# Regrouped units, casting transfers from GpSimd and a new placement in a linear-attention kernel with a bilinear feed-forward

## The chip, the cores and the metric

The kernel runs on one core of one Trainium2 chip, alone. The metric is the device time of one execution in microseconds (us). The engines are named as in the profile: PE (TensorE), DVE (VectorE), ACT (ScalarE), POOL (GpSimd) and SP, which issues transfers.

## The reference, cut to what matters

```python
# q, k, v: (4, 8, 768, 64); lam: (8,)
for b in range(12):                       # blocks of 64 positions
    intra = einsum(qb, kb) * Dmask        # lam ** (i - j) below the diagonal
    intra = einsum(intra, vb)
    inter = einsum(qb * lam_pow, kv_state)
    out[block] = intra + inter
    kv_state = lam_block * kv_state + einsum(kb * rev_pow, vb)
x = out.transpose(0, 2, 1, 3).reshape(3072, 512)
return ((x @ w_a) * (x @ w_b)) @ w_out    # w_a, w_b: 512 x 1536; w_out: 1536 x 512
```

Inputs and output are float32; the kernel computes in bf16 with float32 sums.

## The kernel before, in words

The 3072 tokens are 24 units of 128 tokens, six for each of the four batches. For each unit the kernel loads q, k and v (256 KB each, in rows of 64 numbers), scales q and k by powers of lam (`qk`), turns them (`qkT`, on PE in `piece_T` or by a transposing transfer), makes the scores `kq` of its eight heads in two PSUM banks, multiplies them by a triangular mask into `m`, and adds `m` times v and the running state times q into `o_ps` (`pieces_O`). A copy to `xT` ends the attention of a unit (`evac_o`). The running state `kvd` is kept in PSUM over a batch and copied to `st`. The first four units are loaded packed and handled together at the start (`scale4`, `part_k`, `natural_k`, `scores4`).

The feed-forward works on groups of units, `GROUPS = (4, 1, 2, 4, 4, 4, 4, 1)`. A plain group (`ffn`) makes for each of twelve 128-column chunks f the product with w_a (`a_ps`), copies it to bf16 (`a_sb`), makes the product with w_b (`b_ps`), multiplies both into `ab`, and then multiplies `ab` with w_out (`op`). A group in `Z_GROUPS` (`ffn_z`) uses a scheme with seven half-size products instead of eight. It needs sums of the weights (`wz`, `weight_sum`), sums of `xT` (`x_sums`: `z_sub`, `z_add`, `z_mix`), three combining subtractions on DVE per output pair, copies `u` on ACT, and one product `ab <- oab` per pair. A group in `ZO_GROUPS` also makes the output product in this way (`ab_sum`, `out_half`, 14 halves per group), and these halves run while the next group is in its first product.

The weights come as 18 chunks of 512 KB (six each of w_a, w_b, w_out; `load_w`), are staged in float32 in buffers that later hold other things, and are cast to bf16 by DVE, ACT or POOL (`cast_w`). `pump` issues, on SP's queue, the next transfer for which a buffer is free, in one fixed order for weights and units.

Each engine runs its instructions in program order. That order is written out by hand: the group functions call `hook(slot)` after certain steps, and the table `PLAN` names the pieces that are issued at each slot (P: scale q, k and cast v; T: turn; S: scores and masks; V: state; O2: outputs of two units; X: sums of xT; SM and H: parts of the seven-product output; WS, WO, C: weight sums and casts). Tables such as `SUM_ENG` and `MASK_ACT` choose the engine. An instruction waits on semaphores for what it reads and for the buffers it overwrites, and everything behind it on its engine waits too.

Of the kernel before, what the change touches and what calls it, by code (L numbers as in the profile page):

```python
# [22 lines left out]
def _bc(ap, dims):  # L23
# [4 lines left out]
GROUPS = (4, 1, 2, 4, 4, 4, 4, 1)  # L28
W_CHUNKS = (256,) * 6
W_STEPS = ((0, 1), (2,), (3,), (4, 5))  # L30
W_HALVES = (4, 5)
LOOKAHEAD = {9: 2, 10: 1}
DMA_T = range(7, 24)
KEEP_GROUPS = 2
PACK = 4

PLAN = {
    0: [(7, 'C', 0), (8, 'C', 1), (17, 'C', 2), (18, 'WS', 0), (19, 'WS', 1), (20, 'V', 3),
        (21, 'PK', 4), (22, 'C', 3), (23, 'T', 4), (25, 'C', 4), (27, 'C', 5), (28, 'PV', 4),
        (29, 'WS', 2), (29, 'PK', 5), (31, 'S', 4), (33, 'O', 4), (34, 'WS', 3),
        (35, 'WS', 4), (35, 'V', 4)],
    1: [(0, 'PV', 5), (0, 'WS', 5), (3, 'T', 5), (4, 'PK', 6), (6, 'PV', 6), (9, 'P', 7),
        (11, 'S', 5), (11, 'T', 6), (12, 'S', 6), (13, 'P', 8), (13, 'O2', (5, 6)),
        (13, 'WS', 6), (13, 'WS', 7)],
    2: [(0, 'V', 6), (2, 'W', None), (2, 'W', None), (3, 'P', 9), (4, 'V', 7), (4, 'S', 7),  # L50
        (6, 'V', 8), (10, 'PK', 10), (11, 'PV', 10), (11, 'P', 11), (11, 'W', None),
        (11, 'S', 8), (11, 'P', 12), (12, 'Q', (7, 8, 9, 10)), (13, 'P', 13),
        (13, 'W', None), (13, 'V', 9), (14, 'O2', (9, 10)), (14, 'X', 3), (15, 'W', None)],
    3: [(1, 'S', 11), (5, 'S', 12), (8, 'O2', (11, 12)), (10, 'P', 14), (12, 'S', 13),
        (15, 'P', 15), (17, 'WO', 0), (17, 'S', 14), (18, 'V', 13), (18, 'WO', 1),
        (19, 'P', 16), (19, 'O2', (13, 14)), (20, 'P', 17), (21, 'S', 15), (21, 'P', 18),
        (24, 'WO', 2), (25, 'WO', 3), (25, 'WO', 4), (25, 'X', 4)],
    4: [(0, 'S', 16), (1, 'V', 15), (3, 'S', 17), (4, 'O2', (15, 16)), (4, 'P', 19),
        (6, 'P', 20), (6, 'S', 18), (10, 'O2', (17, 18)), (10, 'X', 5), (11, 'S', 19),
        (13, 'P', 21), (16, 'SM', (4, 0)), (17, 'SM', (4, 2)), (17, 'P', 22), (17, 'S', 20),  # L60
        (17, 'SM', (4, 4))],
    5: [(0, 'SM', (4, 1)), (1, 'H', (4, 0)), (1, 'V', 19), (2, 'O2', (19, 20)),
        (2, 'H', (4, 1)), (3, 'SM', (4, 3)), (4, 'H', (4, 2)), (5, 'S', 21), (5, 'V', 21),
        (6, 'S', 22), (6, 'H', (4, 3)), (7, 'SM', (4, 5)), (7, 'H', (4, 4)),
        (8, 'H', (4, 5)), (9, 'P', 23), (9, 'H', (4, 6)), (9, 'SM', (4, 6)),
        (10, 'SM', (4, 7)), (10, 'H', (4, 7)), (11, 'H', (4, 8)), (11, 'S', 23),
        (12, 'H', (4, 9)), (12, 'SM', (5, 0)), (12, 'H', (4, 10)), (13, 'SM', (5, 2)),
        (13, 'H', (4, 11)), (14, 'O2', (21, 22)), (16, 'H', (4, 12)), (17, 'X', 6),
        (17, 'H', (4, 13)), (17, 'SM', (5, 4))],
    6: [(0, 'SM', (5, 1)), (0, 'O', 23), (1, 'H', (5, 0)), (1, 'SM', (5, 3)),  # L70
        (2, 'H', (5, 1)), (4, 'H', (5, 2)), (5, 'H', (5, 3)), (6, 'SM', (5, 5)),
        (7, 'H', (5, 4)), (7, 'SM', (5, 6)), (8, 'H', (5, 5)), (9, 'SM', (5, 7)),
        (9, 'H', (5, 6)), (10, 'H', (5, 7)), (11, 'H', (5, 8)), (13, 'H', (5, 9)),
        (14, 'H', (5, 10)), (14, 'SM', (6, 0)), (15, 'H', (5, 11)), (15, 'SM', (6, 2)),
        (15, 'SM', (6, 4)), (16, 'H', (5, 12)), (17, 'H', (5, 13))],
    7: [(0, 'H', (6, 0)), (0, 'SM', (6, 1)), (0, 'H', (6, 1)), (0, 'SM', (6, 3)),
        (0, 'SM', (6, 5)), (0, 'H', (6, 2)), (1, 'H', (6, 3)), (3, 'H', (6, 4)),
        (4, 'H', (6, 5)), (5, 'SM', (6, 6)), (5, 'SM', (6, 7)), (5, 'H', (6, 6)),
        (6, 'H', (6, 7)), (6, 'H', (6, 8)), (6, 'H', (6, 9)), (7, 'H', (6, 10)),
        (8, 'H', (6, 11)), (10, 'H', (6, 12)), (10, 'H', (6, 13))],  # L80
}
Z_GROUPS = (3, 4, 5, 6)
ZO_GROUPS = (4, 5, 6)
FIN_AT = 5
N_LATE = 3
EV_ENG = {(u, b): "act" for u in range(24) for b in range(2)}
MASK_ACT = dict(enumerate([0] * 7 +
                        [1] +
                        [0] * 3 +
                        [1] * 2 +  # L90
                        [0] * 4 +
                        [1] * 3 +
                        [0] +
                        [1] +
                        [0] * 2))
KV_ENG = dict(enumerate(["dve"] * 10 + ["act"] * 2 + ["dve"] + ["act"] * 11))
VB_ENG = dict(enumerate(["pool"] * 7 +
                        ["dve"] * 3 +
                        ["pool"] * 5 +
                        ["dve"] * 2 +  # L100
                        ["act"] +
                        ["pool"] +
                        ["dve"] +
                        ["pool"] +
                        ["act"] * 3))
SUM_ENG = {(3, 0): 'dve', (3, 1): 'dve', (3, 2): 'pool', (3, 3): 'dve', (3, 4): 'pool', (3, 5): 'pool', (3, 6): 'dve', (3, 7): 'dve', (4, 0): 'dve', (4, 1): 'pool', (4, 2): 'pool', (4, 3): 'pool', (4, 4): 'dve', (4, 5): 'pool', (4, 6): 'pool', (4, 7): 'pool', (5, 0): 'dve', (5, 1): 'dve', (5, 2): 'pool', (5, 3): 'pool', (5, 4): 'dve', (5, 5): 'pool', (5, 6): 'pool', (5, 7): 'dve', (6, 0): 'pool', (6, 1): 'dve', (6, 2): 'pool', (6, 3): 'dve', (6, 4): 'dve', (6, 5): 'pool', (6, 6): 'dve', (6, 7): 'dve'}
XS_ENG = {(3, 0): 'dve', (3, 1): 'dve', (3, 2): 'dve', (4, 0): 'dve', (4, 1): 'dve', (4, 2): 'dve', (5, 0): 'dve', (5, 1): 'pool', (5, 2): 'pool', (6, 0): 'pool', (6, 1): 'pool', (6, 2): 'pool'}
WS_ENG = {0: 'dve', 1: 'dve', 2: 'dve', 3: 'dve', 4: 'dve', 5: 'dve', 6: 'dve', 7: 'pool'}
WO_ENG = {0: 'dve', 1: 'dve', 2: 'pool', 3: 'dve', 4: 'dve'}
CO_ENG = {0: 'pool', 1: 'pool', 2: 'pool', 3: 'dve', 4: 'dve', 5: 'dve'}  # L110
# [3 lines left out]
def kernel(  # L114
# [40 lines left out]
    raw_pool = ctx.enter_context(tc.tile_pool(name="raw", bufs=1))  # L155
# [16 lines left out]
    def z_bank(name, i):  # L172
        return ps_pool.tile([128, 2, 256], F32, name=name, tag=f"ps{i}")
# [5 lines left out]
    raw = {}  # L179

    def load_x(w, u):
        b, nb = divmod(u, NB)
        if w == "v" and u == GROUPS[0] - 1:
            t = o_pool.tile([128, H, D], F32, name="vf", tag="osb")
        else:
            t = ld_pool.tile([128, H, D], F32, name=w + "f", tag=w + "f")
        nc.sync.dma_start(out=t, in_={"q": qr, "k": kr, "v": vr}[w][b, nb])
        raw[u, w] = t
# [7 lines left out]
    staged = {}  # L196
    HN, NP = d_model // 2, FC // 2

    def sum_tile(shape, dt, name, tag):
        return sum_pool.tile(shape, dt, name=name, tag=tag)  # L200

    ab_stage = ab_pool.tile([128, 3, 1024], F32, name="wst", tag="ab")
    slots = [lambda: oab_pool.tile([128, 1024], F32, name="wst", tag="oab")] * 2
    slots += [lambda i=i: ab_stage[:, i] for i in range(3)]
    slots += [lambda t=t: sum_tile([128, 1024], F32, "wst", t) for t in ("zab", "wy0", "wy1")]
    once = lambda: xT_pool.tile([128, 1024], F32, name="wst", tag="xT")
    slots.insert(0, once)
# [8 lines left out]
    def load_w(kind, c):  # L216
        slot = slots.pop(0)
        t = slot()
        if kind == "o":
            t = t.rearrange("p (k n) -> p k n", k=2)  # L220
            nc.sync.dma_start(out=t, in_=wo_r[:, 2 * c:2 * c + 2, :])
        else:
            w = W_CHUNKS[c]
            t = t[:, :KS * w].rearrange("p (k n) -> p k n", k=KS)
            r = wa_r if kind == "a" else wb_r
            if c in W_HALVES:
                t = t.rearrange("p k n -> p (k n)").rearrange("p (k n) -> p k n", k=2)
            nc.sync.dma_start(out=t, in_=w_part(r, c))
        staged[kind, c] = t, slot

    def cast_w(kind, c, eng):
        t, slot = staged.pop((kind, c))
        if slot is not once:
            slots.append(slot)
        if kind == "o":
            dst = wo_sb[:, 2 * c:2 * c + 2, :]
        else:
            dst = w_part(wa_sb if kind == "a" else wb_sb, c)
        if eng == "act":
            nc.scalar.copy(dst, t)  # L240
        elif eng == "pool":
            nc.gpsimd.tensor_copy(dst, t)
# [59 lines left out]
    def pump():  # L302
        while pending:
            kind, c = pending[0]
            if kind in "abo":
                if not slots:
                    return
# [771 lines left out]
```

## Time and profile before

| | |
|---|---|
| times of three runs | 225.08, 225.38, 226.76 us; median 225.38 |
| span of the profiled execution | 224.7 us |
| PE busy, matmuls | 214.6 us, 2235 |
| DVE, ACT, POOL busy | 164.8, 123.2, 101.1 us |
| packets and bytes of all transfers | 99081, 39.42 MB |
| granted PE clock | 1.00 in all slices |

The profile gives the span of one execution, from the first instruction to the last; what lies around it is the difference to the measured time, some 0.7 us against the median. Busy time counts the union of an engine's instructions. Matmuls overlap in the pipeline, so that the distance between the starts of two of them, not the length of one, is PE's pace.

### The profile page before, as it was taken

To read this page: it belongs to the slowest core of one execution; us is meant where nothing else is said; L and a number is where in the kernel's file an instruction comes from. 1 tells how busy PE (TensorE), PEld (TensorE's weight loads), DVE (VectorE), ACT (ScalarE), POOL (GpSimd) and SP (SyncE) were. 2 spreads that over 40 slices of the span, in tenths; PEclk is the share of its full clock that TensorE was granted. 3 is DMA by queue.
4 is the path that set the end of the run, shared out by engine and by line. 5 is a ranking of instruction groups with operands and counts; after the bars stand their busy time and mean duration, and the time that the engine had idled before them with its cause. 6 is when DMAs were issued, how large, how long until landed. Compare 5 with 4: busy or idle time off the path is not lost.

```text
span 224.7 us, 5609 instructions
## 1 busy us (share of the span) xinstructions
PE 214.6 (96%) x2235; PEld 158.8 (71%) x2235; DVE 164.8 (73%) x269; ACT 123.2 (55%) x251; POOL 101.1 (45%) x95
## 2 busy tenths in 40 slices
PE   7699999989989999999999999899999999999994
PEld 2375444437768757887547878688888888887994
DVE  1895673599699659989878999968686765777440
ACT  3586446017544247775366988776536665533322
POOL 6061004256895075541459359786417722052000
PEclk9999999999999999999999999999999999999999
DMA  4999999998999999999999999652021100112042
GB/s 137 316 231 356 356 384 346 276 217 192 229 198 218 219 180 240 204 253 247 175 240 243 243 206 202 138 98 48 2 88 55 50 1 4 47 48 95 0 143 93
DMA packets 99081, 39.42 MB, mean 175 GB/s; under 512 B 85488, under 2 KB 95088, under 8 KB 99056
## 3 DMA queue, kind: packets, MB, share of 16 engines
q1 hardware_dynamic: 98768, 39.00, 78.0%
q8 instruction: 17, 0.28, 0.5%
q10 hardware_dynamic: 288, 0.07, 0.1%
q14 instruction: 8, 0.07, 0.1%
HBM read 28.32 MB, written 6.29 MB: 154 GB/s over the span
## 4 chain that ended last, share of the span: by engine, by line
PE 80%; DVE 6%; DMA 6%; ACT 3%; issue 2%; SPq 1%; ACTq 0%; DVEq 0%
PE U L730 17%; PE op L852 12%; PE b_ps L596 9%; PE op L643 8%; PE V L730 8%; PE a_ps L596 8%; PE op L792 5%; PE W L730 4%; DMA wst<-in_moe_w_b_dram 4%; PE o_ps L497 3%; DMA k<-in_k_dram 3%; PE kq L457 2%; PE kvd L527 1%; SPq L350 1%; DVE m L480 1%
## 5 line engine op out<-in xcount | busy, mean ns | idle before, releaser
L811 ACT COPY u<-U 128x512 f32<-128x512 f32 x48 | 28.4, 591 | 16.9 <-PE U L730 16.6
L401 POOL TENSOR_TENSOR qk<-kf,lp_k 128x512 bf16<-128x512 f32 x18 | 19.8, 1099 | 34.6 <-DMA kf<-in_k_dram 23.1
L623 DVE TENSOR_TENSOR ab<-a_sb,b_ps 128x128 bf16<-128x128 bf16 (+2 forms) x48 | 19.2, 417 | 14.0 <-ACT a_sb L605 11.1
L480 DVE TENSOR_TENSOR m<-kq,lotri 128x512 bf16<-128x512 f32 x40 | 25.7, 684 | 3.8 <-PE kq L457 3.6
L596 PE MATMUL a_ps<-xT,wa_sb 128*128 128x128 bf16 (+2 forms) x200 | 27.8, 268 | 0.6 <-ACT xT L520 0.5
L596 PE MATMUL b_ps<-xT,wb_sb 128*128 128x128 bf16 (+2 forms) x192 | 27.5, 272 | 0.7 <-ACT oab L736 0.5
L738 DVE TENSOR_TENSOR ab<-oab 128x1024 bf16<-128x1024 bf16 x24 | 18.4, 767 | 10.5 <-ACT oab L736 10.5
L401 POOL TENSOR_TENSOR qk<-qf,lp_q 128x512 bf16<-128x512 f32 x20 | 25.2, 1259 | 1.2 <-DMA qf<-in_q_dram 1.2
L605 ACT CAST a_sb<-a_ps 128x128 bf16<-128x128 f32 (+2 forms) x48 | 17.1, 375 | 14.4 <-PE a_ps L596 14.3
L643 PE MATMUL op<-wo_sb,ab 128*128 128x512 bf16 (+2 forms) x120 | 22.8, 337 | 0.2 <-DVE wo_sb L254 0.2
L596 PEld LDWEIGHTS <-wa_sb 128*128 128x128 bf16 x200 | 16.6, 98 | 6.6 <-issue 0.7
L596 PEld LDWEIGHTS <-wb_sb 128*128 128x128 bf16 x192 | 15.7, 98 | 7.3 <-DVE wb_sb L251 0.7
L730 PEld LDWEIGHTS <-wz_a 128*128 128x128 bf16 x192 | 18.2, 98 | 3.6 <-issue 0.7
L730 PEld LDWEIGHTS <-wz_b 128*128 128x128 bf16 x192 | 18.7, 98 | 2.2
L730 PE MATMUL U<-xT,wz_a 128*128 128x256 bf16 x96 | 18.3, 272 | 0.0
L730 PE MATMUL U<-xT,wz_b 128*128 128x256 bf16 x96 | 18.3, 272 | 0.0
L520 ACT CAST xT<-o_ps 128x512 bf16<-128x512 f32 (+1 forms) x24 | 12.2, 556 | 10.7 <-PE o_ps L497 10.5
L420 POOL CAST vb<-vf 128x512 bf16<-128x512 f32 x14 | 10.9, 778 | 13.9 <-DMA vf<-in_v_dram 13.9
L769 DVE TENSOR_TENSOR oab<-U,u 128x512 bf16<-128x512 f32 x24 | 16.4, 682 | 0.4 <-PE U L730 0.4
L730 PEld LDWEIGHTS <-wa_sb 128*128 128x128 bf16 x144 | 13.4, 97 | 4.5 <-issue 1.7
L643 PEld LDWEIGHTS <-ab 128*128 128x128 bf16 x120 | 10.1, 98 | 8.6 <-issue 0.3
L736 ACT CAST oab<-U 128x512 bf16<-128x512 f32 x24 | 14.2, 591 | 3.6 <-PE U L730 3.5
(126 smaller groups left out, 453.8 us busy)
## 6 DMA issues: line engine op xcount, KB each, us to landing
vf<-in_v_dram SPq DMA_DIRECT2D x24, 256.0 KB, 4.8
qf<-in_q_dram SPq DMA_DIRECT2D x20, 256.0 KB, 4.6
kf<-in_k_dram SPq DMA_DIRECT2D x20, 256.0 KB, 4.6
out_dram<-o_sb SPq DMA_DIRECT2D x18, 256.0 KB, 2.5
wst<-in_moe_w_a_dram SPq DMA_DIRECT2D x6, 512.0 KB, 8.5
wst<-in_moe_w_b_dram SPq DMA_DIRECT2D x6, 512.0 KB, 9.0
wst<-in_moe_w_out_dram SPq DMA_DIRECT2D x6, 512.0 KB, 10.6
out_dram<-o_kept SPq DMA_DIRECT2D x5, 256.0 KB, 4.4
```

What stands on the lines that cost most here:

```text
L401: eng_of(eng).tensor_mul(dst.rearrange("p (c b) d -> p b c d", b=2), x[:].rearrange("p (b c) d -> p b c d", b=2), lp.rearrange("p (b c) o ...
L480: nc.vector.tensor_mul(m, kq[i], lotri_bc)
L596: nc.tensor.matmul(ps[:, lo:hi], lhsT=w_sb[:, s, f * 128:(f + 1) * 128], rhs=xT[:, s, lo:hi], start=(s == 0), stop=(s == KS - 1), skip_gro ...
L605: nc.scalar.copy(a_sb[:, :gt], ps[:, :gt])
L623: nc.vector.tensor_mul(ab[:, f, :gt], a_sb[:, :gt], ps[:, :gt])
L643: nc.tensor.matmul(op[:, lo:hi], lhsT=ab[:, f, t * 128:(t + 1) * 128], rhs=wo_sb[:, f, lo:hi], start=(f == 0), stop=(f == FC - 1))
L730: nc.tensor.matmul(ps[:, k, :], lhsT=wt[:, s, n * 128:(n + 1) * 128], rhs=rhs[i][:, s, :], start=(fresh and k == 0 and s == 0), stop=True, ...
L736: nc.scalar.copy(oab[:, 0], U)
L738: nc.vector.tensor_mul(ab[:].rearrange("p (h i) (t c) -> p h i t c", h=2, t=2)[:, :, n], o5[:, :, :, 0, :], o5[:, :, :, 1, :])
L769: nc.vector.tensor_sub(oab[:, 1], U, v1)
L811: nc.scalar.copy(t, ps)
L852: nc.tensor.matmul(ps[:, t, :], lhsT=lhs[p][:, n, t * 128:(t + 1) * 128], rhs=rhs[:, n, :], start=fresh, stop=True, skip_group_check=True)
```

## The change

- The groups become 4, 1, 3, 4, 4, 4, 4 units. The group of three units uses the seven-product scheme for a and b (with 192-column operands) and the plain output product; the four groups of four use it for both. No plain group stands at the end. The plain group of one unit packs four chunks into each PSUM bank.
- Weights go straight from float32 in memory to bf16 in place, by transfers that cast, issued by POOL (`load_w`); only the first two chunks of w_a still come as float32 on SP's queue and are cast by ACT and POOL (`load_first`, `cast_first`). v of units 4 to 23 comes in the same way as bf16 (`load_x`); v of units 0 to 3 is cast by DVE or POOL. There is no staging and no `pump`: each load is a piece with a place of its own.
- In the first group the products of chunks 0 and 1 are made in two halves, for units 0, 1 and units 2, 3 (`ffn_first`).
- Loads of q and k for units 4 to 6 wait for a one-element memset on DVE (`GATED`).
- Every piece is placed anew, also those of the first four units: `PLAN` has entries for the start (-1) and for each group, with up to 6 slots per output pair (3 before), and finer pieces (LQ, LK, LV, LW: loads; PK, PQ: scaling; TR: turn; S, M: scores, masks; V, K: state and its copy; O, E: outputs and their copy; MU: the product of an output pair, `times`). One table, `VAR`, chooses among variants of a piece: 12 of the 30 products MU go to POOL; twelve units make their scores in quarters of the array (`scores`, 64 x 64 at a time); mask variants copy the scores to bf16 on ACT first and multiply in place on DVE.

```diff
-GROUPS = (4, 1, 2, 4, 4, 4, 4, 1)
+GROUPS = (4, 1, 3, 4, 4, 4, 4)
+Z_GROUPS = (2, 3, 4, 5, 6)
+ZO_GROUPS = (3, 4, 5, 6)
...
-Z_GROUPS = (3, 4, 5, 6)
-ZO_GROUPS = (4, 5, 6)
...
     def load_x(w, u):
         b, nb = divmod(u, NB)
+        if w == "v" and u >= n0:
+            t = prep_pool.tile([128, H, D], BF16, name="vb", tag="vb", bufs=N_VB)
+            nc.gpsimd.dma_start(out=t, in_=vr[b, nb])
...
+            if u in GATED:
+                nc.vector.memset(t[0:1, 0, 0:1], 0.0)
+            nc.sync.dma_start(out=t, in_={"q": qr, "k": kr, "v": vr}[w][b, nb])
...
+    def load_w(x):
+        kind, c = x
+        if kind == "o":
+            nc.gpsimd.dma_start(out=wo_sb[:, 2 * c:2 * c + 2, :], in_=wo_r[:, 2 * c:2 * c + 2, :])
+        else:
+            w, r = (wa_sb, wa_r) if kind == "a" else (wb_sb, wb_r)
+            nc.gpsimd.dma_start(out=w_part(w, c), in_=w_part(r, c))
...
+        step = 64 if var("S", u) else 128
         for hp in range(HP):
-            for i in range(2):
+            for j in range(0, 128, step):
+                for i in range(2):
...
+        if n_act == 2:
+            for i in range(2):
+                nc.scalar.copy(ms[i], kq[i])
+            nc.vector.tensor_mul(m, m, lotri_all)
...
+    def ffn_first(x):
+        kind, f, part = x
+        gt = n0 * BLK
+        lo, hi = ((0, gt // 2), (gt // 2, gt), (0, gt))[part]
...
+    def times(x):
+        g, n = x
+        hw = outs[g]["hw"]
+        o5 = oabs[x][:].rearrange("p (h t) k c -> p h t k c", h=2)
+        dve_pool("MU", x).tensor_mul(
...
+    def cast_first(x):
+        c, k0, k1, lo, hi = x
+        dst, src = wa_sb[:, k0:k1, 256 * c + lo:256 * c + hi], first[c][:, k0:k1, lo:hi]
```

The new plan of the first group, as far as the prediction speaks of it (the kind and number after FF are w_a or w_b and the chunk f; the last number is the half, or 2 for all):

```python
(-1, 'FF', ('a', 0, 0)), (-1, 'LW', ('b', 4)), (-1, 'FF', ('a', 1, 0)), (-1, 'FF', ('a', 1, 1)),
(-1, 'FF', ('a', 0, 1)), (-1, 'FF', ('b', 0, 0)), ..., (-1, 'FF', ('a', 2, 2)), ..., (-1, 'FF', ('a', 7, 2)),
(-1, 'FF', ('a', 6, 2)), (-1, 'FF', ('a', 3, 2)), ..., (-1, 'FF', ('b', 0, 1)), (-1, 'FF', ('b', 6, 2)),
(-1, 'FF', ('b', 7, 2)), ..., (-1, 'FF', ('b', 1, 0)), (-1, 'FF', ('b', 1, 1)), ..., (-1, 'FF', ('a', 9, 2)),
(-1, 'FF', ('a', 11, 2)), (-1, 'FF', ('a', 10, 2)), (-1, 'FF', ('a', 8, 2)), (-1, 'FF', ('b', 11, 2)), ...
```

POOL issues the weight chunks in the order b0, a3, b3, a5, a4, b4, b5, b1, a2, o0, o1, b2, o2, o4, o3, o5 (a3 is chunk 3 of w_a, which holds f = 6 and 7; chunks 4 and 5 are the upper and lower half of the rows for f = 8 to 11).

## The prediction

> **What bounds the kernel now.** I read the page's busy shares first, then its chain, then the chain in order of time for TensorE's pace, then stretches of time and groups of instructions. Busy shares and chain on the page:
> ```profile
> PE 214.6 (96%) x2235; PEld 158.8 (71%) x2235; DVE 164.8 (73%) x269; ACT 123.2 (55%) x251; POOL 101.1 (45%) x95
> ...
> PE 80%; DVE 6%; DMA 6%; ACT 3%; issue 2%; SPq 1%; ACTq 0%; DVEq 0%
> ```
> TensorE (PE) is nearly always busy and is 80% of the chain. Its busy time holds pipeline tails, so I took its pace from the chain in order of time (start, length, what):
> ```profile
> 13.76 7.88 DMA wst<-in_moe_w_b_dram
> 21.66 0.44 DVE wb_sb L251
> 22.14 3.63 PE b_ps L596 x16
> 25.77 1.73 PE a_ps L596 x8
> ...
> 55.14 0.45 PE tps L443 x8
> ...
> 144.57 0.66 PE op L852 x6
> ```
> Eight 512-column matmuls follow each other in 1.73 us, 0.216 us each; six of 256 columns in 0.66 us, 0.109 each; eight of 128 in 0.45 us, 0.056 each. So an unhindered matmul costs its columns and nothing else. I gave every matmul of the trace this pace (half for one that uses half of the rows or half of the columns of the array, since two such run side by side) and compared with the distance to the next start. The span then splits into: 1.3 us before the first matmul, 199.3 us of paced matmuls, 21.0 us in which PE stood, and 3.1 us from the start of the last matmul to the end (copy and store). Of the 21.0 us standing, 7.1 lie in the first 20 us (loads and scaling of the first four units) and 13.9 later. Of these 13.9, eight places of 0.3 us or more hold 4.7 us: near 21.6, 45.0, 46.1, 63.7, 85.5, 142.0, 171.3 and 203.9 us. The rest are about 0.1 us each, many at a change of matmul form.
>
> Two stretches (start:end, length, then busy time and count of PE, PEld, DVE, ACT, POOL, clock, DMA share, GB/s) and three rows of groups show what else is close:
> ```profile
> 18.00:40.00 22.00, 21.80 (x110) 10.30 (x108) 12.63 (x22) 11.98 (x19) 3.80 (x5) 1.00 1.08 354
> ...
> 119.00:152.00 33.00, 32.12 (x391) 26.06 (x390) 29.22 (x44) 26.51 (x54) 24.68 (x18) 1.00 0.95 183
> ```
> ```profile
> L472 DVE TENSOR_TENSOR m<-raw_kq,lotri 128x512 bf16<-128x512 bf16 x7 | 5.6, 804 | 0.2
> ```
> ```profile
> L706 POOL TENSOR_TENSOR z_add<-xT 128x1024 bf16<-128x1024 bf16 x2 | 5.2, 2608 | 2.6 <-ACT xT L520 2.6
> ...
> L705 POOL TENSOR_TENSOR z_sub<-xT 128x1024 bf16<-128x1024 bf16 x1 | 2.1, 2127 | 1.4 <-ACT xT L520 1.4
> ```
> In 18 to 40 us the weights stream at 354 GB/s, so one chunk of 524288 bytes takes 1.48 us, while PE does 20.7 us of first-step products (96 x 0.216). In 119 to 152 us VectorE (DVE) is busy 29.2 of 33 us: the second limit. The clock is 1.00 throughout.
>
> **The change, part by part.** (1) *Groups 4,1,3,4,4,4,4 instead of 4,1,2,4,4,4,4,1.* Three units that ran the plain product now form a seven-product group with 192-column operands; the first full seven-product group also gets the seven-product output. Counting both instruction lists without the warm-up: 512 columns 220 to 176, 256 columns 1048 to 1040, 192 columns 0 to 168, 128 columns 360 to 224; the narrow state updates rise by 32 of about 0.014 us. A 192-column matmul has only four warm-up rows here, so I bound it by 0.056 and 0.109 and take the middle, 0.083, since the pace is linear. Sum: -44 x 0.216 - 8 x 0.109 + 168 x 0.083 - 136 x 0.056 + 32 x 0.014 = -9.5 - 0.9 + 13.9 - 7.6 + 0.5 = **-3.6 us**, all on PE, the engine that sets the end. The bounds of the 192 row make it -8.1 to +0.8. Some score products are cut into quarters of the array: twice as many, the same paced time.
>
> (2) *Weights by GpSimd's casting transfers.* Off go 12 weight copies on DVE (eight of about 0.69 and four of 0.42 us, 7 us), five on ScalarE (4.8 us), five on GpSimd. On GpSimd come 16 weight issues and 20 v issues, and 14 v casts of 0.61 us go. The trace shows no issue from GpSimd and no casting transfer. SP's issue takes 0.46 us (lower end); if the issue is as slow as the chunk on the wire it is 1.48 us (upper end); I take 1.0, between them. For the wire time the lower end is half a chunk, 0.74 us, if the bytes written counted, the upper end 2.96 us if the cast halved the rate; I take 1.48, since the bytes read are the same. Cover: the first step starts at 18.15 us now and I leave it there. GpSimd gets to its first weight issue after a mask product and a v cast, about 16.3 us, so chunk b0 lands near 20.0 and is wanted after a0 and a1 at 19.9: 0 to 1 us of waiting. Then the wanted times, in the order of the plan: a3 21.2, b3 24.2, a4 and a5 26.8, b4 and b5 30.3, b1 32.0, a2 34.6. At 1.48 us a chunk they land at 21.5, 23.0, 25.9, 28.9, 30.4, 31.8. So +0.5 us, and the pace at which the plan breaks is about 1.7 us a chunk ((26.8 - 20.0) / 4). Behind a late issue on GpSimd stand the k and q scalings of unit 4, and behind those only the group-1 scores at the end of stage 0. SP loses 36 issues; its transposes and k, q loads move up, which the cover of ten us of output products in stage 0 hides.
>
> The skill speaks against this part. The Trainium skill, SBUF — State Buffer, section "SBUF: two separate sides", says that a DVE copy in its two-port mode keeps GpSimd from writing descriptors, and gives about 620 ns growing to 3100 ns for one transfer. By that figure 36 issues could cost an estimated 89 us of GpSimd time in the worst case; but the copies that do it are the ones taken away here, three are left, so by the rule too it is near nothing. No run here shows it yet.
>
> (3) *Pieces placed anew.* The plan now has six slots in each output pair instead of three, and nothing stays at the eight places above: weight casts on DVE ahead of PE (21.6, 46.1), the scaling of unit 4 (45.0), the group 1 and 2 boundaries (63.7, 85.5), the first output pairs of a group (142.0, 171.3) and the last plain group (203.9). If all go and the small waits stay: -4.7. If all come back elsewhere: 0; if the places of the longer plan are worse by as much: +4.7; if only form changes remain (about 5 us): -8. I take **-4.7**.
>
> (4) *Load of the other engines.* With each group's undisturbed duration the DVE list comes to 167 us before and 173 after: the casts go, 18 more combining subtractions come (of 2 x 192 columns, about 0.54 between the 0.41 and 0.68 of 256 and 512 columns), and masks of 1024 columns. ScalarE 134 to 136. GpSimd 95 to 129, of which 12 products of the output pairs, priced at 2.1 to 2.6 us by the L705 and L706 rows, and 36 us are issues. None passes PE's 196, so 0; but DVE in the stages of 1 to 5 now has 117 us of work beside PE's 120 (a stage's wait on DVE is the third rival).
>
> (5) *End.* The last group ends on its own seven products, with the last half sorted by token tile and stored in two pieces of 128 KB, where the last stores were 64 KB: +0.2 us. Its 14 half products (14 x 0.66 = 9.2 us) cover the sums except for about one wait, as now.
>
> Sum on the profiled execution: 224.7 - 3.6 + 0.5 - 4.7 + 0.2 = 217.1 us of span. The median of three runs is 225.4, 0.7 above the span; with it **217.8 us**.
>
> **The rivals.** *A. Forecast*, 213 to 222: PE's work falls by 3.6 and the named waits go. *B. The placement is much better*: waits after 20 us fall to the form changes, 5 of 13.9 us: 217.8 - 4.2 = 213.6, and with the first 20 us tightened by the finer plan, 210. For: the first 20 us have 7.1 us of standing PE. Against: they wait on loads (k lands at 10.3) that are not moved. *C. DVE and GpSimd take it back.* The L472 row is 410 ns undisturbed in its shortest of seven and 804 in the mean: beside a GpSimd tensor instruction DVE with two operands from SBUF waits. DVE's instructions lost about 12 us to this before. With 12 GpSimd products of 2.1 to 2.6 us, an increase by half costs 6 us: 217.8 + 6 = 224, no change. For: DVE was at 29.2 of 33 us. Against: total GpSimd tensor work hardly grows (92 to 93 us). The same skill page and section calls this an exclusive lock; the row agrees (1292 ns at most against 410). *D. Casting transfers come late*, the slower side. If a chunk takes 2.96 us on the wire or on GpSimd's queue, b0 is 1.6 us late and, each wait put off onto the later wants, a3 1.7, a4 3.3, b5 2.4, b1 1.3, a2 0.3: 10.6 us with PE standing in the first step, 10 more than the 0.5 above: 217.8 + 10 = 228. It decides from 1.7 us a chunk; at 2.2 it is about 4 us. For: no cast is shown in the trace, and SP's queue had the rate at 1.48. Against: the bytes read stay, and the slack was there. *E. The change does less than it says* (PE's list shorter, but the 192-column product as dear as 256): -3.6 becomes +0.8: 222.
>
> **How the numbers follow.** A 0.60, B 0.13, C 0.09, D 0.14, E 0.04. About 1% (2.3 us) is what a measurement of this kernel tells from no change. Faster than 223.1: A, B, most of E and a quarter of C: 0.77. Within 1%: the rest of C and the mild end of D: 0.10. Slower: the rest of D and some of C: 0.13. The predicted time is A's, 217.8. The range reaches into B and into the mild half of D: 210 to 227; A's own is 213 to 222.
>
> **What would show it.** Paced matmul time 195.7 us; PE's standing after 20 us below 10 us; b0 landing by 20 to 21 us and no wait for wa_sb or wb_sb above 0.5 us; GpSimd issues near 1 us; no DVE busy share above 85%. It is wrong if PE waits for weight transfers between 20 and 40 us (D), if the two-operand DVE rows lengthen and PE stands for oab, m or z sums (C), or if the U rows of 192 columns follow at 0.109 us (E).

## The result, and the profile after

The changed kernel takes 238.83 us (median of four runs, 238.72 to 241.34); the kernel before took 225.23 us beside it. The ratio is 1.061, with a 95% interval of 1.0545 to 1.067: slower, where 217.8 us was forecast. The profiled execution has a span of 237.0 us, against 224.7. Times and ratios below leave out runs of a kernel that are over 1.5% longer than its fastest, so that one kernel keeps a single run and has no ratio, and the profiles of three (v transfers later, eight products, v by casting transfers in the kernel before) are of such longer runs.

The page after (busy shares, granted clock by slice, shares of the chain):
```profile
PE 215.6 (91%) x2343; PEld 162.6 (69%) x2343; DVE 169.6 (72%) x267; ACT 124.5 (53%) x246; POOL 113.8 (48%) x110
...
PEclk9999999999999999999999999997999999999999
...
PE 31%; DVE 2%; ACT 0%; issue 0%
```
PE's share fell from 96% to 91%, and one slice has a lower clock. The chain follows back only to 157 us, where it ends on a DVE sum (`z_add`). The two stretches shown in the prediction, now (start:end, length, busy time and count of PE, PEld, DVE, ACT, POOL, clock, DMA share, GB/s):
```profile
18.00:40.00 22.00, 19.96 (x140) 10.59 (x134) 8.14 (x20) 8.95 (x16) 13.91 (x18) 1.00 1.24 186
119.00:152.00 33.00, 29.18 (x360) 23.53 (x359) 26.78 (x39) 20.52 (x43) 18.86 (x13) 1.00 0.72 116
```
In the first, DVE and ScalarE have lost the weight casts, as meant, and PE is busy only 1.8 us less; in the second PE stands 3.8 us while DVE and GpSimd are both *less* busy than before. Busy shares do not say what PE waited for.

I split the span as in the prediction: paced matmuls, and PE's standing by place and size (us). "Small" holds all waits under 0.3 us after 20 us, and time lost to a lower clock.

| | paced | first 20 us | waits of 0.3 and more, 20 to 50 us | the same, after 50 us | small | last matmul to the end |
|---|---|---|---|---|---|---|
| before | 199.3 | 7.1 | 1.6 | 3.1 | 9.2 | 3.1 |
| after | 195.8 | 7.9 | 2.0 | 12.8 | 13.1 | 4.2 |

The differences are -3.5 + 0.8 + 0.4 + 9.7 + 3.9 + 1.0 = 12.3 us, the whole of 237.0 - 224.7. Three waits make 7.8 of the 12.8: 2.28 us at 106.6, 2.81 at 133.1, 2.67 at 157.9.

The third wait. DVE's and GpSimd's timeline after (start, length, instruction):
```profile
155.74 0.68 DVE L898 TENSOR_TENSOR oab<-W,u 128x512 bf16<-128x512 f32 x1
156.34 0.67 DVE L982 TENSOR_TENSOR o_sb<-op,u 128x512 f32<-128x512 f32 x1
156.94 3.67 DVE L809 TENSOR_TENSOR z_add<-xT 128x1024 bf16<-128x1024 bf16 x1
```
```profile
154.22 1.05 POOL L502 TENSOR_TENSOR qk<-kf,lp_k 128x512 bf16<-128x512 f32 x1
155.21 2.70 POOL L347 DMA_DIRECT2D vb<-in_v_dram  x3
157.90 2.15 POOL L822 TENSOR_TENSOR ab<-oab 128x1024 bf16<-128x1024 bf16 x1
```
z_add takes 0.68 us alone. Here it ends 0.56 us after GpSimd's unbroken run of a scaling, three v issues and an output-pair product. By these records it would have been done at 157.62, 0.28 us before the product starts. The wait has a second price (stretches as above):
```profile
158.00:161.00 3.00, 0.50 (x6) 0.31 (x4) 3.00 (x2) 0.23 (x1) 2.04 (x1) 1.00 1.48 164
...
163.00:164.00 1.00, 1.00 (x7) 0.69 (x6) 0.84 (x2) 0.00 (x0) 0.00 (x0) 0.50 0.36 107
...
166.00:170.00 4.00, 4.00 (x51) 3.35 (x50) 2.33 (x5) 2.85 (x7) 1.74 (x2) 1.00 0.97 222
```
From 161.7 the granted clock is 0.50 for 3.41 us: 1.7 us more. The first two waits are another thing: ScalarE's copies u want a buffer that a kept output tile still holds (waits: us in total, times, longest), and SP issued that store late, behind a transpose that waited for qk:
```profile
ACT u L913 <- DMA out_dram<-o_kept: 6.9, 3, 3.4
```
```profile
122.77 0.91 SPq L355 DMA_DIRECT2D kf<-in_k_dram  x1
131.53 1.23 SPq L517 DMA_TRANSPOSE qkT<-qk  x1
132.81 0.58 SPq L706 DMA_DIRECT2D out_dram<-o_kept  x1
```

### The profile page after: what moved, and what is told of

Read it like the earlier page. It is cut to its first block, busy times and chain, and to the rows that moved or that the text cites. A ratio compares the mean times of both kernels' runs of the same rounds, so it can differ in the third digit from the quotient of the medians.

```text
span 237.0 us, 5770 instructions
## 1 busy us (share of the span) xinstructions
PE 215.6 (91%) x2343; PEld 162.6 (69%) x2343; DVE 169.6 (72%) x267; ACT 124.5 (53%) x246; POOL 113.8 (48%) x110
## 5 line engine op out<-in xcount | busy, mean ns | idle before, releaser
L913 ACT COPY u<-U 128x512 f32<-128x512 f32 (+1 forms) x60 | 34.3, 572 | 40.6 <-PE U L851 32.2
L851 PEld LDWEIGHTS <-wz_a 128*128 128x128 bf16 x240 | 22.3, 98 | 13.1 <-issue 6.1
L822 POOL TENSOR_TENSOR ab<-oab 128x1024 bf16<-128x1024 bf16 (+1 forms) x12 | 24.8, 2065 | 13.3 <-ACT oab L857 6.8
L719 PE MATMUL op<-wo_sb,ab 128*128 128x512 bf16 x96 | 22.6, 380 | 0.7 <-DVE ab L822 0.7
L851 PE MATMUL U<-xT,wz_a 128*128 128x256 bf16 (+1 forms) x120 | 22.6, 270 | 0.2 <-ACT u L913 0.2
L891 DVE TENSOR_TENSOR oab<-U,u 128x512 bf16<-128x512 f32 (+1 forms) x30 | 19.7, 656 | 4.3 <-PE U L851 4.1
L851 PE MATMUL U<-xT,wz_b 128*128 128x256 bf16 (+1 forms) x120 | 22.5, 269 | 0.0
L963 PEld LDWEIGHTS <-ab 128*128 128x128 bf16 x192 | 18.9, 99 | 2.9 <-issue 0.2
L913 ACT COPY u<-V 128x512 f32<-128x512 f32 (+1 forms) x30 | 17.2, 575 | 4.8 <-DMA out_dram<-o_kept 2.6
L963 PE MATMUL op<-wy,ab 128*128 128x256 bf16 x144 | 19.5, 279 | 0.0
L347 POOL DMA_DIRECT2D vb<-in_v_dram x20 | 18.3, 919 | 1.2 <-DMA wb_sb<-in_moe_w_b_dram 1.2
L719 PEld LDWEIGHTS <-ab 128*128 128x128 bf16 x96 | 8.8, 98 | 10.7 <-DVE ab L822 0.9
```

Source lines behind the costliest of these rows:

```text
L347: nc.gpsimd.dma_start(out=t, in_=vr[b, nb])
L719: nc.tensor.matmul(op, lhsT=ab[:, f, t * 128:(t + 1) * 128], rhs=wo_sb[:, f, :], start=(f == f0), stop=(f == f1))
L822: dve_pool("MU", x).tensor_mul(outs[g]["ab"][:].rearrange("p (h i) x -> p h i x", h=2)[:, :, n, :2 * hw] .rearrange("p h (t c) -> p h t c" ...
L851: nc.tensor.matmul(ps[:, k, :], lhsT=wt[:, s, n * 128:(n + 1) * 128], rhs=rhs(i)[:, s, :], start=(fresh and k == 0 and s == 0), stop=True, ...
L891: nc.vector.tensor_sub(oab[:, 1], U, v1)
L913: nc.scalar.copy(t, ps)
```

## The experiments

Theory 1: PE's new standing is a sum of separate late waits. Theory 2: the wire as a whole is late. Theory 3, formed after the first four runs: DVE is held by GpSimd's runs. (Where eight products or the pairs go to DVE, "Theory 1" stands for its rival that DVE is short of time.) Each kernel is given with its ratio to the kernel before on the same chip (226.2 to 226.7 us there), and kernels from different chips are compared by these ratios.

**Kept stores earlier.** `(1,'W',0) (4,'W',1) (6,'W',2) (8,'W',3)` in stage 1 and `(4,'W',4)` in stage 2, instead of (9) in stage 1, (17) and (26) in stage 3, (14) and (20) in stage 4.

> The stores of the five kept output tiles (pieces W) move from stages 1, 3 and 4 to the first slots of stage 1 and slot 4 of stage 2; nothing else moves. Theory 1 (separate late waits: the new standing of TensorE is a sum of single waits, and each goes when its own cause goes): the copies u no longer wait for a buffer that a kept store holds, so the 2.3 us near 106.6, the 2.8 us near 133.1 and the 0.6 us near 137 go, and the time falls by 4.5 to 6 us, from 238.8 to about 233.5. Theory 2 (the transfers as a whole are too many for the wire, and whatever is served earlier makes something else later): the 1.25 MB moved forward push k and q loads back by some 5 us of wire time, new waits come in stages 1 and 2, and the time stays within 1.5 us of 238.8.

242.2 us, ratio 1.068 [1.062, 1.075]. The copies u no longer wait, as Theory 1 said, but new waits came: 2.65 us at 61.1 for a transposed qk, 2.37 at 73.9 for an oab, and where 2.81 us had gone near 133 stood 3.13 at 140.0 for another DVE result. Theory 1 falls as a count of independent waits; what the stores met at their new places was not taken apart.

**One product to DVE.** `-('MU', (4, 5)): 1` in VAR.

> One product of the output pairs, the last of the group of stage 4, goes from GpSimd to DVE. Theory 1a (GpSimd's tensor instruction holds DVE's sum z_add): z_add, 3.67 us from 156.94, falls to 1.0 to 1.7 us (only the last transfer issue, 157.01 to 157.90, lies beside it), the wait of 2.67 us at 157.9 shrinks to under 0.9, and if the stretch of half clock behind it (3.4 us, about 1.7 us of time) is a result of this wait it goes too: 235 to 237. Theory 1b (the transfer issues hold it as well, one after the other until 157.9): the same within 0.3 us, with z_add ending at 158.4 or later. Theory 2 (nothing single): the wait reappears within the next pairs because DVE is 0.8 to 1.2 us longer, and the time is 238 to 239.5.

236.8 us, 1.045 [1.040, 1.051]. z_add (one line further up) now overlaps transfer issues alone:
```profile
156.32 0.68 DVE L808 TENSOR_TENSOR z_add<-xT 128x1024 bf16<-128x1024 bf16 x1
```
So with the product gone the same issues do not hold it: the hold hangs on the product behind them. No half clock follows.

**v transfers later.** LV 22, 21, 20 from slots 1, 2, 2 of stage 5 to 5, 7, 8.

> The three v transfers of units 20 to 22 move from slots 1 and 2 of stage 5 to slots 5, 7 and 8, so that their issues (155.2 to 157.9) no longer stand on GpSimd ahead of and beside z_add; the product stays on GpSimd. If transfer issues alone hold DVE: z_add takes 0.7 to 1.3 us, the wait of 2.67 us goes, 235 to 236.5. If the product holds it (Theory 1a): the product starts as soon as its operand is there, about 156.8, and holds z_add until about 159, so that 1.0 to 1.5 us of the 2.67 stay: 236 to 238. Theory 2: 238 to 239.5.

239.8 us, 1.059 [1.047, 1.070], above the 236 to 238 expected for that case. z_add took 2.61 us, held by the product alone, and PE waited 1.61, close to what was expected; but three other waits of 2.3 to 3.1 us were each followed by 3.41 us of half clock, and nothing was won.

**Kept stores by ScalarE.** `-nc.sync.dma_start(out=out_r[row], ...)`, `+nc.scalar.dma_start(...)` in store_kept.

> The five kept stores stay at their places in the plan but are issued by ScalarE instead of SP. Theory 1 (the stores are late because they stand in SP's queue behind transposes that wait for their operand, 7.5 and 7.8 us): the stores of stage 4 go out some 5 us earlier and the wait of 2.8 us near 133 goes; near 106.6 the copy u comes within 2 to 3 us of the issue, so that wait halves at best; ScalarE has five issues more (0.4 to 1.1 us each by SP's rows). In all 2 to 4 us less, 235 to 237. Theory 2 (the wire is what is late): landing stays 3.5 us or more after the issue, and the time stays at 238 to 239.5.

236.6 us, 1.043 [1.035, 1.051]: within the expected 235 to 237. The copies u wait no more for a kept store, so SP's queue made the stores late. But PE still stands 2.94 us at 134.2, now for this (DVE, then GpSimd):
```profile
132.75 3.90 DVE L822 TENSOR_TENSOR ab<-oab 128x1024 bf16<-128x1024 bf16 x1
```
```profile
130.90 1.65 POOL L934 TENSOR_TENSOR zab<-ab 128x768 bf16<-128x768 bf16 x1
132.48 0.94 POOL L347 DMA_DIRECT2D vb<-in_v_dram  x1
133.45 1.65 POOL L934 TENSOR_TENSOR zab<-ab 128x768 bf16<-128x768 bf16 x1
135.05 1.04 POOL L502 TENSOR_TENSOR qk<-kf,lp_k 128x512 bf16<-128x512 f32 x1
```
A product of 0.68 us starts during a v issue and ends 0.56 us after *two* further GpSimd instructions. Every variant so far had this wait; the kept store had only covered it in the changed kernel. Hence Theory 3.

**Less tensor work on GpSimd.** Eight MU out of VAR; then, with the kept stores on ScalarE, the same and all SM and X.

> Eight of the twelve products of the output pairs that GpSimd has now go to DVE; the other four, the sums and all places stay. Theory 3 (a DVE instruction with both operands in SBUF that meets GpSimd work waits until the unbroken run of GpSimd work ends; z_add took 3.68 us in three runs with the product there and 0.68 with it gone): z_add takes 0.68 us, its wait of 2.67 us and the half clock behind it go as in the run with one product moved; the wait near 134 stays, since sums and a scaling hold the product there (3.47 us with the last product gone): 234 to 236.5, or 1.0 to 1.5 us better than that if more products on the path are freed. Theory 1 (DVE is short of time): its busy time rises by about 5.5 us (8 of 0.68), and the time is 238 to 241.

> The same eight products, all twelve sums SM and the two sums X that GpSimd has go to DVE, and the kept stores are issued by ScalarE (236.6 us with that alone). GpSimd keeps the scalings of q and k, four products and the transfers. Theory 3: with the kept stores out of the way the waits of 2.9 us (near 134) and 2.7 us with 1.7 us of half clock (near 156) go, and the time is 229 to 232. Theory 1: DVE's busy time rises by about 14 us (8 of 0.68, 12 of 0.55, 2 of 0.7) less 8 or so of holding; if DVE is short of time, new waits for oab and ab come in the stages 4 to 6 and the time is 236 to 240.

The first: 236.4 us; z_add took 0.68 us, but the ab product was held 4.90 us at 133.3 by an issue and three GpSimd instructions. The second: 236.6 us, 1.046 [1.040, 1.051], not the 229 to 232 expected: two scalings behind a v issue hold the product as well (2.82 us at 128.9, PE stands 2.92). So scalings behind the issue hold DVE as sums and products do.

**The casting transfers alone, in the kernel before.** In one kernel 14 of the 18 weight chunks (all but a0, a1, b0, b1) by `nc.gpsimd.dma_start(out=w_part(w, c), in_=w_part(r, c))`, their casts gone, and the q and k loads of unit 4 held until the third step; in another v of units 4 to 23 by `nc.gpsimd.dma_start(out=t, in_=vr[b, nb])`, with six buffers.

> The kernel before, with one part of the change: fourteen of the eighteen weight chunks (all but a0, a1, b0, b1) come by GpSimd's casting transfers, issued one after the other once the first chunks are cast, and their copies on DVE, ScalarE and GpSimd go; q and k loads of unit 4 are held until the third step. If a casting chunk keeps the 1.48 us of the plain one: the waits of 0.44 us at 21.6 and near 46 go and nothing is late: 224 to 225.5. If it takes 1.6 to 2.1 us also without k and q loads beside it: a3, a4 or a5 are late, 1 to 3 us of waiting in the first step: 226 to 228.5.

> The kernel before, with the other part: v of units 4 to 23 comes by GpSimd's casting transfers (issues of about 0.92 us), and the twenty copies to bf16 (on GpSimd, DVE and ScalarE) go. If such an issue does not hold DVE (z_add took 0.68 us beside one): DVE and ScalarE have less to do, GpSimd 8 to 10 us more, and the time is within 1 us of before, 224 to 226.5. If it holds DVE, or if v lands late because GpSimd comes late to its issue: 227 to 230.

Weights: 1.002 [0.998, 1.0065], no difference. v: 236.1 us, 1.040 [1.031, 1.049], with a DVE sum of 0.94 us taking 5.67 at 123.6, through a scaling, a v issue and a sum. So 9 us of loss come with v alone, in a kernel that had none of the regrouping. Holding DVE is not all of it: PE's longest wait there, 3.15 us at 102.3 with 3.41 us of half clock behind it, is for a copy u whose buffer a kept store frees, and that store landed 7.1 us after its issue (4.5 in the kernel before). Why it landed late was not tested.

**The four late v transfers apart.** LV 20 to 23 to the head of stage 4 behind LV 19, where GpSimd then waits for q; kept stores by ScalarE; in the second also the product (4, 5) on DVE.

> Compared with the run whose kept stores ScalarE issues (236.6 us). The four v transfers of units 20 to 23 move to the start of stage 4, right behind that of unit 19, where GpSimd then waits for q; nothing else. Theory 3 (a transfer issue inside an unbroken run of GpSimd work holds a waiting DVE instruction to the end of the run; seen at 132.8 and 154.8 us of that run): the product near 133 takes at most 1.4 us instead of 3.90, its wait of 2.9 us goes; z_add, now beside one GpSimd product only, takes about 2.6 us as in the run with v moved behind it, and its wait falls from 2.7 to about 1.6; with the half clock 231 to 233.5. Theory 2 (the wire): half a megabyte moved forward makes q and k of stage 4 late by 2 us, the wait moves to qk, 235 to 238.

> The same, and the last product of the group of stage 4 goes from GpSimd to DVE, so that z_add meets no GpSimd work. Theory 3: both waits (2.9 and 2.7 us) and the stretch of half clock (1.7 us) go: 228.5 to 231.5. Theory 2: 235 to 238.

230.2 us, 1.0195 [1.016, 1.023]; and 1.014 [1.004, 1.023]. By the ratios, moving four issues wins some 5 us against the kernel with the kept stores alone (1.043): the 2.94 us wait becomes 1.04, z_add's 1.61, and no half clock comes. Of Theory 2's lateness one wait appeared in the first, 1.27 us at 169.0 for a transposed qk.

**Tiny issues, in the kernel before.** 13 transfers of 128 x 4 elements that nobody reads, `nc.gpsimd.dma_start(out=tiny_sb[:, c:c + 4], in_=wo_r[:, 0, c:c + 4])`, first between k and q scaling, then behind the v copy.

> The kernel before, with one tiny casting transfer more (128 x 4 elements that nobody reads) on GpSimd between the k scaling and the q scaling of each of units 11 to 23: 13 issues that add nothing to the wire. Theory 3: a DVE instruction with both operands in SBUF that is waiting when such an issue runs stays held until the q scaling ends, 1.5 to 2.3 us in several of the 13 places (0.8 to 1.3 us there in the kernel before): DVE's holding rises by 3 us or more and the time by 1 to 4 us. Theory 4 (an issue costs GpSimd's own time alone, 13 x 0.8 us on an engine 45% busy, or it is the wire that made the v transfers dear): within 0.7 us of before.

> The kernel before, with the same 13 tiny transfers issued after the v copy of the unit, at the end of GpSimd's run or behind it. Theory 3: an issue that ends a run holds nothing (DVE got in during it in the runs so far), so DVE's holding and the time stay within 0.7 us of before. Theory 4: the same as the kernel with the issues inside, within 0.5 us of it.

Inside: 233.0 us, 1.033 [1.026, 1.041]. After: 1.006 [1.002, 1.011]. The same 13 issues cost some 7.5 us or 1.5, by their place alone. Most of the 7.5 lies at one of the 13 places: PE stands 3.23 us at 123.0 for the sum below, and 6.83 us of half clock begin before that wait ends, some 2.9 us more. Inside, DVE's worst case and GpSimd beside it:
```profile
121.16 5.01 DVE L714 TENSOR_TENSOR z_mix<-xT 128x512 bf16<-128x512 bf16 x1
```
```profile
119.11 1.58 POOL L407 TENSOR_TENSOR qk<-kf,lp_k 128x512 bf16<-128x512 f32 x1 [2.07 <-DMA kf<-in_k_dram]
120.64 0.59 POOL L264 DMA_DIRECT2D tiny_sb<-in_moe_w_out_dram  x1
121.25 1.05 POOL L407 TENSOR_TENSOR qk<-qf,lp_q 128x512 bf16<-128x512 f32 x1
122.24 0.61 POOL L426 CAST vb<-vf 128x512 bf16<-128x512 f32 x1
122.81 3.07 POOL L296 TENSOR_TENSOR wy<-wo_sb 128x1536 bf16<-128x1536 bf16 x1
```
A sum of 0.41 us starts in the 0.59 us issue and waits through three GpSimd instructions. Theory 3 holds for runs with an issue in them.

**What is left.**

> The changed kernel with the kept stores on ScalarE (236.6 us), and the v transfers of units 4 to 23 left out: these units use v of unit 3, so the output is that of other data. It shows what the twenty transfers cost in all, by their issues, by holding DVE and by their 2.6 MB on the wire. If holding DVE inside runs is nearly all of it: the two waits near 134 and 156 and the half clock go, as with v moved, and GpSimd is 18 us freer: 228 to 231. If the wire or the issues themselves cost as much again: 223 to 227.

> Compared with the run whose four late v transfers come early and whose product of stage 4 is on DVE (230.1 and 227.9 us undisturbed). Three transfers more are moved: the weight chunks a5 and a4 are issued before GpSimd waits for the cast of chunk a1 (they were issued 20.7 to 22.1, after that wait), and the v transfers of units 12 and 16, the two that still stood inside a run of GpSimd work, go behind others. If the first step's waits come from the issue's place on GpSimd: the wait of 1.5 to 2.0 us near 28.5 goes, the product near 106 (2.31 us) takes 0.7 to 1.3, and the time is 226.5 to 228.5. If the weights are late by the wire (chunks land 1.6 to 2.1 us apart whatever their issue): the wait moves to b4, b5 or a2 and the time is 228.5 to 230.5.

> The version with all moves so far, and seven more products, the twelve sums SM and the two sums X of GpSimd go to DVE. If what is left to win is DVE held by GpSimd's tensor instructions (12 us of holding in all): 1 to 3 us less than the version without this. If DVE, with some 12 us more to do, is short of time in the stages 3 to 6: 1 to 4 us more than it.

Without v transfers (the units then use unit 3's v) 229.0 us, 1.010 [1.006, 1.0145]: by the ratios 7.4 us below the kernel with the kept stores on ScalarE, and 2.1 below the one with four issues moved. As those four only changed places, where the issues stand, and with it holding DVE, was most of the cost. Its waits after 50 us are 6.2 us (before 3.1), its small ones 12.1 (before 9.2); of these 1.5 stand for seven matmuls that are missing from its trace (2336 records against 2343). Its two longest waits, 1.62 us at 151.8 and 1.33 at 131.9, again follow DVE instructions that GpSimd's tensor work held (z_add 2.62 us, a product 2.12), here with no issue near. More moves did not help: 1.028 [1.019, 1.038], where the weight wait stayed at 1.28 us and one of 2.52 came at 36.3, PE waiting for unit 4's scaling; and 1.0685 [1.058, 1.079], where DVE's holding was least of all (7.5 us in sum) but PE waited 3.23 us for a scaling and 4.91 for a transposed qk. No version beat the kernel before.

## Why the prediction was wrong

*Term 1 (PE's work, -3.6)* was right: -3.5 paced. *Term 5 (end, +0.2)* was 1.0 in truth, and the first 20 us, left as they were in the sum, took 0.8 more.

*Term 2 (casting transfers, +0.5)* was right for the weights: PE waited 2.0 us in the first step, 0.4 more than before, and alone they cost nothing. (The two waits, 0.72 and 1.30 us for chunks of w_a, are above the 0.5 us that was named as a sign; the sum came out because the old waits of this stretch went.) The sizes were off: chunks landed from 20.75 to 52.22 us, 16 of them, 2.10 us apart with k and q beside them, not 1.48; that is the pace of rival D, at 4 us by its working, but the first step took little harm. The issue took 0.73 to 0.78 us in the mean of each weight, for v 0.92, not 1.0. It failed for v, which I costed as GpSimd's own time and no more: 9 us in the kernel before (1.040), 7.4 here.

*Term 4 (engine load, 0)* is the step that failed with it. Rival C had the mechanism, DVE with two SBUF operands held by GpSimd, and I gave it 0.09, at 224 us, because GpSimd's tensor time hardly grew. The sum was the wrong measure: DVE's holding (time beyond the shortest of the same shape, both operands in SBUF) rose from 10.0 us only to 13.9. What changed is that the longest single holds grew from 0.9 us to 3.0, on instructions that PE waits for, one with a stretch of half clock behind it. That an issue inside a run lengthens the hold was in no term and no rival.

I had let the Trainium skill, SBUF — State Buffer, section "SBUF: two separate sides", speak against the transfers by its sentence on DVE copies that keep GpSimd from writing descriptors. The traces show the reverse: v issues kept to 0.88 to 0.95 us in the changed kernel, and DVE was the one to wait. The same section's lock, held by a GpSimd instruction for the whole of that instruction, fits where no issue stood ahead in GpSimd's run (208 held DVE instructions, 1.95 us at most); with one ahead, the hold could go on past that instruction.

*Term 3 (placement, -4.7)* failed too. The old places gave way to others: the kept stores in SP's queue cost 2 to 4 us (1.061 to 1.043), and even with them and the v transfers out of the way the standing after 20 us is some 5.0 us above the kernel before, where 4.7 less was forecast. The two longest waits left, 1.62 and 1.33 us, stand behind held DVE instructions, which is rival C without any issue; the others, up to 1.1 us each at many places, were not taken apart, and the cause of most of that remainder stays open.

## What to carry to other kernels

Before a transfer goes to GpSimd's queue, read what GpSimd does right behind the issue and which DVE instruction with both operands in SBUF starts meanwhile: put the issue last in a run, ahead of a wait. An issue does not cost its 0.6 to 0.9 us; it costs what PE stands for the DVE result, and another 1.7 us or more if the clock falls after that. A wait that covers another hides it: take one away and look at what ends last there then.

## What the runs showed of the hardware

GpSimd instructions less than 0.1 us apart are called one run here, and a DVE instruction with both operands in SBUF is called held when it took 0.15 us or more beyond the shortest of its shape. Over all traces of the case, 208 were held with no issue ahead of them in the run: each through one GpSimd tensor instruction, 1.95 us at most, and where an issue came next (52 of them) DVE was let in beside it. Thirteen were held through two or three tensor instructions, 1.1 to 4.7 us, and all 13 had an issue ahead in the same run. In 15 cases a DVE instruction clearly outlasted an issue that a tensor instruction followed at once, and stayed held until that one had ended or one behind it (1.2 to 4.7 us). Two others, begun 0.45 us before such an issue's end, took their 0.68 us unhindered, so not every such meeting holds. I know of no reason for it; the runs show only the order.

In 15 of 22 waits of PE of 2.2 us or more, half clock for 3.41 us (four times 6.83) began during the wait or within 1.4 us of its end; no run without such a wait had any before the last stores. The length of the wait alone does not decide: 2.30 us was followed by half clock, 3.13 was not. The Trainium skill, TensorE: Matmul & The Clock Gate, section "Part 1: The HAM clock gate (the "warmup" mystery)", has a free-running window of about 3.4 us and names a whole idle window as what lowers the clock; the length agrees, but here 2.30 us of standing was enough.
